# Reordering the loads, writes and small matmuls at the start of a fused SSM-convolution and GeGLU kernel

## The chip, the cores and the metric

The kernel runs on one core of a Trainium2 chip. The metric is the device time of one execution in microseconds (us); less is better. The kernel before was timed three times: 909.62, 912.13 and 916.34 us, median 912.13. One more execution was profiled.

## What is computed

Two layers, one after the other, are each applied twice to x (2048 tokens by 576 channels, bf16): a gated long convolution and a feed-forward block. Cut to what matters:

```python
def _A_ref(q, k, v, shift_k, ssm_k, ssm_D):       # q is layernorm(x)
    k_shift = sum over t of k delayed by t, times shift_k[:, ks - 1 - t]     # ks = 4 taps
    kv = k_shift * v
    y = irfft(rfft(kv, 2S) * rfft(ssm_k, 2S))[:S]  # causal convolution along the tokens, per channel
    return q * (y + kv * ssm_D)

def _B_ref(x, w_gate, w_up, w_down):              # 576 -> 4608 -> 576
    return (gelu(x @ w_gate) * (x @ w_up)) @ w_down

x = A_q
x = x + _A_ref(layernorm(x), A_k, A_v, A_shift_k, A_ssm_k, A_ssm_D)
x = x + _B_ref(layernorm(x), B_w_gate, B_w_up, B_w_down)
x = x + _A_ref(...); x = x + _B_ref(...)
```

The convolution y does not depend on x, so it is computed once and used by both layers.

## The kernel before, in words

**Tiling.** Tokens are worked on in four blocks of 512. The convolution of a block is done by transforms that are matmuls with tables of cosines and sines (W, Wx); the product with the transformed filter stands in between, on VectorE (DVE). Filter block b is needed from token block b on. The feed-forward block runs in units (layer, token block), each in three phases of 12 feature tiles; weights for the gate and up products come in groups of four tiles (a group, wgu, is three loads: L1193 to L1195), down weights in halves of a phase (wd, L1203). TensorE (PE) carries nearly everything.

**Who orders the work.** Each engine runs its instructions in program order. The start (function begin, L831 to L1130) is written out by hand. After it a planner takes over: it keeps a model of the engines' times (Pace) and, between the feed-forward products, calls fill (L1420), which hands out the waiting convolution steps, loads and writes as the model says that they are ready. Loads and writes are issued by SP (nc.sync) and by POOL (nc.gpsimd), a few small ones by ACT (nc.scalar); each of these queues issues in order, and a DMA that has to wait holds up all that stand behind it on the same queue.

**The start.** SP loads k, the first filter block hn, v, the tables, x_b (L863 to L875), and then weight groups 0 and 1 (L876, head.more(1)). ACT loads the taps as one row, sk1 (L862), and the vector D as one row, dvec (L864). TensorE turns the tap row into columns with twelve matmuls of one column each (L891), which become wcol (L894); from wcol DVE and ACT make diagonal matrices dg, and with them the shift of k by its taps is done on TensorE (shift_taps, L818). The last 192 channels are shifted on DVE instead (L943 to L949) with sx, the taps broadcast by two matmuls (L906, L909). D becomes columns by five one-column matmuls (L915), goes to dcol (two copies, L933 and L934) and is added to the filter's first tap (L939). Then k*v (L991) and the first filter block (hT0) are transformed (L219, L228), multiplied (kacc) and transformed back (L415).

**The second filter block.** It has to be turned so that its time steps lie on the partitions. Four transposing DMAs read it from DRAM into hx[:, 0] (L977); SP then issues weight group 2 (L978, head.more(2)), writes hx[:, 0] to DRAM (Td, L979), and reads it back in another order into hx[:, 1] (L981). The tile hx takes over the place of kT, the shifted k's operand, so the first transpose waits for kT's last reader. Its transform (L282) is put between the feed-forward products by the planner; the first of these comes after the seventh product of the first unit.

**Writes and POOL's queue.** put(kt, ...) writes transformed blocks to DRAM, h0[kt] to Hd and kc[kt] to Kd (spill, L425): put(0, h0, kc), put(2, h0), put(2, kc), then the taps' broadcast skc (L1083), k of token block 1 (load_k(1), L1084), put(1, h0, kc), put(3, h0), v of block 1 (L1094), put(3, kc). They are read again in the steps of later token blocks (kr, hr; L547, L555).

**The first unit.** The first unit's first phase is done in two halves of 256 tokens, six products (half_gu, L1673, 36 matmuls each) per half, since token tiles 0 and 2 are normalised first. first_half (L1601) does the six products of tiles 0 and 2; after the third and the fourth of them (n = 2 and 3) tiles 1 and 3 are turned (turn0, nine transposes on TensorE, L1478) and copied by ACT (copy0, two copies, L1485), for the second half. The fifth product is the first to use weight group 2, the third the first to use group 1. Products n < 4 are finished by a Gelu on ACT and a multiplication on DVE (L1678, L1679); later ones by two ACT instructions (hidden, L1652 and L1653) and a multiplication over two products on DVE (L1656). PSUM pairs of the products come from a pool of three, in turn; the turnings take from the same pool.

Of the kernel before, what the change touches and what calls it, by code (L numbers as in the profile page):

```python
# [18 lines left out]
BF16 = mybir.dt.bfloat16  # L19
# [3 lines left out]
P = 128  # L23
# [63 lines left out]
class Conv:  # L87
# [743 lines left out]
    def begin(self, head, tables):  # L831

        tc, nc, D, KS = self.tc, self.nc, self.D, self.KS
        nd = D // P
        width = lambda db: min(P, D - db * P)
        with ExitStack() as es:
            tmp = es.enter_context(tc.tile_pool(name="s_tmp", bufs=1))
            AT = 96
            sk1 = tmp.tile([AT + 1, D, KS], BF16, name="sk1")
            dvec = tmp.tile([1, D], BF16, name="dvec")  # L840
            dcol = tmp.tile([P, nd + 1], F32, name="dcol")
            nt = nd - 1
            DW = D - nt * P
# [13 lines left out]
            full = wx[1][:].rearrange("p i c -> p (i c)")[:, 0:256]  # L857

            nc.vector.memset(full, 1.0)
            nc.vector.memset(ones[:], 1.0)  # L860
            nc.vector.memset(sk1[0:AT, nt * P:, :], 0.0)
            nc.scalar.dma_start(out=sk1[AT:AT + 1, :, :].rearrange("p d j -> p (d j)"), in_=self.sk.rearrange("d j -> (d j)").unsqueeze(0))  # L862
            self.load_k(0, nc.sync)  # L863
            nc.scalar.dma_start(out=dvec[:], in_=self.sD.unsqueeze(0))  # L864
            nc.vector.memset(kT[:, :, :, 0:2], 0.0)
            nc.vector.memset(below[:, 0:1], 0.0)
            nc.vector.tensor_copy(out=below[:, 1:P], in_=self.ident[:, 0:P - 1])
# [5 lines left out]
            head.more(0)  # L873
            nc.sync.dma_start(out=self.Wx[:], in_=tables[:, 24:26, :])
            nc.sync.dma_start(out=self.W[:, 12:24, :], in_=tables[:, 12:24, :])  # L875
            head.more(1)  # L876

            new = lambda: self.psp.tile([P, 2, 512], F32, tag="pr", name="ps")
            small = lambda: self.cpsp.tile([P, 2, 512], F32, tag="cps", name="cps")
# [6 lines left out]
            idle = small()  # L886
            busy(idle, 8)
            ps = new()
            for db in range(nt):
                for j in range(KS):  # L890
                    nc.tensor.matmul(ps[:, 0, db * KS + j:db * KS + j + 1], lhsT=sk1[AT:AT + 1, db * P:(db + 1) * P, j],  # L891
                                     rhs=ones[AT:AT + 1, 0:1],
                                     start=True, stop=True)
            nc.vector.tensor_copy(out=wcol[:].rearrange("p b j -> p (b j)"), in_=ps[:, 0, 0:nt * KS])  # L894

            def diagonals(db, js=range(KS)):
                for j in js:
# [13 lines left out]
            rest = slice(nt * P, D)  # L911
            px = new()
            at = DW
            for db in range(nd + 1):
                nc.tensor.matmul(px[0:width(db), 1, at + db:at + db + 1], lhsT=dvec[:, db * P:db * P + width(db)], rhs=ones[0:1, 0:1],  # L915
                                 start=True, stop=True)
            for i in range(KS - 1):
                nc.tensor.matmul(px[:, i // 2, i % 2 * DW:(i % 2 + 1) * DW], lhsT=below[:], rhs=k[:, RT - KS + 1 + i, rest],
                                 start=True, stop=True)
# [2 lines left out]
            for n, dbs in enumerate(DBS):  # L922
                pt = new_t() if n else small_t()
                pts.append(pt)
                for e, db in enumerate(dbs):
                    for u in range(RT):
                        nc.tensor.transpose(pt[:, e, u * P:(u + 1) * P], k[:, u, db * P:(db + 1) * P], self.ident[:])
            nc.scalar.copy(out=kx[:, 0:2, :], in_=px[:, 0, 0:2 * DW].rearrange("p (i c) -> p i c", c=DW))
            nc.scalar.copy(out=kx[:, 2, :], in_=px[:, 1, 0:DW])
            for dbs, pt in zip(DBS, pts):  # L930
                ne = len(dbs)
                if dbs is DBS[1]:
                    nc.scalar.copy(out=dcol[:, 0:nd], in_=px[:, 1, at:at + nd])  # L933
                    nc.scalar.copy(out=dcol[0:D - nd * P, nd:nd + 1], in_=px[0:D - nd * P, 1, at + nd:at + nd + 1])  # L934
                nc.scalar.copy(out=kT[:, dbs[0]:dbs[-1] + 1, :, 2:P + 2],
                               in_=pt[:, 0:ne, 0:RT * P].rearrange("p e (u q) -> p e u q", u=RT))

# [37 lines left out]
            hx = head.scratch([P, 2, RT, D], "hx")  # L975
            for i in range(RT):
                nc.sync.dma_start_transpose(out=hx[:, 0, i:i + 1, :], in_=self.hk[:, BS + i * P:BS + (i + 1) * P])  # L977
            head.more(2)  # L978
            nc.sync.dma_start(out=self.Td[1].rearrange("(t p) d -> p t d", p=P), in_=hx[:, 0])  # L979
            self.hT1 = hx[:, 1]  # L980
            nc.sync.dma_start(out=self.hT1, in_=self.Td[1].rearrange("(p i) d -> p i d", i=RT))  # L981
            skT = tc.dram_tile([1, KS * D], BF16, name="skT")
# [1 line left out]
            def taps_out():  # L984
                for j in range(KS):
                    nc.gpsimd.tensor_copy(out=self.skc[AT:AT + 1, j, :], in_=sk1[AT:AT + 1, :, j])
                nc.gpsimd.dma_start(out=skT[:], in_=self.skc[AT:AT + 1, :, :].rearrange("p j d -> p (j d)"))
            for dbs, o in zip(DBS, out):
                ne = len(dbs)
                vd = v[:, :, dbs[0] * P:(dbs[0] + ne) * P].rearrange("p i (e c) -> p e i c", e=ne)  # L990
                tt(out=vd, in0=o[:, 0:ne], in1=vd, op=ALU.mult)  # L991
# [29 lines left out]
            def put(kt, *what):  # L1021
                for w in what:
                    self.spill((self.Kd if w is kc else self.Hd)[0][kt], w[kt])
                self.flush(0.0)
# [56 lines left out]
            whole(1, 1)  # L1081
            kfwd(1, 1, new())
            nc.gpsimd.dma_start(out=self.skc[:].rearrange("p j d -> p (j d)"), in_=skT[:].broadcast_to([P, KS * D]))  # L1083
            self.load_k(1, nc.gpsimd)  # L1084
            apart(1, 0)
            apart(1, 1)
            kacc(1)
            put(1, h0, kc)
            put(3, h0)
            head.even_out(0)  # L1090
            kfwd(3, 0, small())
            head.even_out(2)
# [11 lines left out]
            for j in (0, 2):  # L1104
                head.gate_even(j, Y[j])
                head.mean(j)
            put(3, kc)
            for j in (0, 2):
                head.sq(j)
                head.std(j)  # L1110
# [16 lines left out]
            head.stats(3)  # L1127
            head.gate(1, None, 0)
            self.A0 = A
            self.startup = False  # L1130


@with_exitstack
def ssm_geglu_kernel(ctx, tc, A_q, A_k, A_v, A_shift_k, A_ssm_k, A_ssm_D, B_x, B_w_gate, B_w_up,
# [53 lines left out]
    def load_wgu(n):  # L1188
        if n >= NWB * GP:
            return  # L1190
        f0 = (n % NG) * fw
        w = wpool.tile([P, NKC, fw], BF16, tag="wgu", name="wgu")
        nc.sync.dma_start(out=w[0:HK, :, :], in_=wg_v[:, :, f0:f0 + fw])  # L1193
        nc.sync.dma_start(out=w[HK:P, 0:NKC - 1, :], in_=wu_v[:, 1:NKC, f0:f0 + fw])
        nc.sync.dma_start(out=w[HK:P, NKC - 1:NKC, :], in_=wu_v[:, 0:1, f0:f0 + fw])  # L1195
        wgu[n] = w
# [248 lines left out]
    with tc.manual_schedule():  # L1445
# [24 lines left out]
        def turn0(j, other=None):  # L1470
            if 0 not in xnT_of:
                xnT_of[0] = xtp.tile([P, NKC, CH], BF16, tag="xnT", name="xnT")
            if j not in turned:
                reserve0(j, other)
            pt = turned[j]
            for b in range(NKC):
                c0 = b * P if b < 5 else HK + (b - 5) * P
                nc.tensor.transpose(pt[b // 5][:, b // 5, (b % 5) * P:(b % 5 + 1) * P], xn0[j][:, c0:c0 + P], ident[:])  # L1478
# [103 lines left out]
        def more(k):  # L1582
            if k == 0:
                load_x(0, nc.sync)
            elif k == 1:
                for n in range(2):
                    load_wgu(n)
            else:
                load_wgu(2)
        head = SimpleNamespace(  # L1590
            zero=neghalf_t[:], more=more, reserve=reserve0, idle=idle0, stats=stats0, act_stats=act_stats0, half_stats=half_stats0, root_of=root_of0, mean_of=mean_of0, scales=scales0, even_out=even_out0, gate_even=gate_even0, gate=gate0, mean=mean0, sq=sq0, std=std0, norm=norm0, turn=turn0, copy=copy0,
            scratch=lambda shape, name: xtp.tile(shape, BF16, tag="xnT", name=name),
# [8 lines left out]
        def first_half(hT):  # L1601

            gvars[0][1]["rstd"] = small.tile([P, 1], F32, tag="e_rstd", name="rstd")
            nc.vector.reciprocal(out=gvars[0][1]["rstd"][:], in_=gvars[0][1]["std"])
            gate0(1, None, 1)
            mean0(1)
            gate0(3)
            mean0(3)
            for n in range(FP // 2):
                tail = half_gu(hT, n, 0, n < 4)  # L1610
                t.pe += C_GU
                if n == 3:
                    t.on_dve(C_HT, t.on_act(C_GELU, t.pe + 0.15) + 0.15)
                if n == 0:
                    sq0(1)
                    root0(1)
                    norm0(1)
                if n < 4:
                    tail()
                if n == 1:  # L1620
                    sq0(3)
                    load_x(1)
                    root0(3)
                elif n in (2, 3):
                    if n == 2:
                        norm0(3)
                        for part, kt in ((1, 0), (0, 1), (1, 1)):
                            conv.apart0(conv.A0, part, kt)
                        conv.together0(conv.A0)
                        t.dve, t.act = t.pe + 2.4, t.pe + 0.6  # L1630
                    conv.run_p()
                    j = 2 * n - 3
                    turn0(j)
                    copy0(j, nc.scalar.copy)
                    t.on_act(1.4, t.pe)
                if n > 3:
                    tail()
                if n == 4:
                    t.dve -= EARLY
                if n > 1:  # L1640
                    fill(t.pe + C_GU + HURRY, False, True)
# [67 lines left out]
        for wb, ph, ui, first, final in visits:  # L1709
# [27 lines left out]
            if wb == 0:  # L1737
                first_half(hT)
                for n in range(FP // 2):
                    tail = half_gu(hT, n, 1, False)  # L1740
                    t.pe = max(t.pe, free.popleft()) + C_GU
                    free.append(tail())
                    if n == 0:
                        conv.window = t.pe + 0.6
                    if n % 2:
                        when_due(t.pe, load_wgu, n // 2 + 3)
                    fill(t.pe + lead(FP // 2 - 1 - n), now(), conv.left > 0)
# [135 lines left out]
```

## Time and profile before

| | |
|---|---|
| median of three runs | 912.13 us |
| profiled execution, its own time | 916.24 us |
| its span, first to last instruction | 914.3 us |
| PE busy | 902.3 us, 99% of the span |
| DVE, ACT, POOL busy | 63%, 36%, 18% |
| weight loads of PE (PEld) busy | 57% |
| DMA | 132.90 MB, mean 145 GB/s |

Times in the profile are counted from the span's start. A row of the list of waits has who waited, for what, the total in us, how often, and the longest. A row of the timeline has start, length, engine, line, operation and tiles; in brackets the idle time before it and what ended it. The list of DMA issues gives the size of each and the median time from issue to landing. The chain of work that ended last is followed back from the last instruction, each step to what released it.

### The profile page before, as it was taken

How to read it: one execution, taken by the hardware profiler on the slowest of the kernel's cores; microseconds unless marked ns; L12 is line 12 of the kernel's file. 1: busy time of each engine (PE TensorE's matmuls, PEld its weight loads, DVE VectorE, ACT ScalarE, POOL GpSimd, SP SyncE). 2: the span in 40 equal slices, each digit the busy share in tenths (PEclk: the TensorE clock that was granted, in tenths of full speed). 3: DMA queues.
4: the chain of work that ended last, by engine and by line, in shares of the span. 5: the costliest groups of instructions: out<-in, count | busy, mean ns of one | idle time of the engine just before them, and what ended most of it. 6: DMA issues, size and time to landing. Idle time of an engine off the chain costs nothing.

```text
span 914.3 us, 19185 instructions
## 1 busy us (share of the span) xinstructions
PE 902.3 (99%) x8143; PEld 525.5 (57%) x8143; DVE 576.8 (63%) x985; ACT 328.9 (36%) x618; POOL 160.2 (18%) x339
## 2 busy tenths in 40 slices
PE   9979999999999999999999999999999999999998
PEld 7766556465565564664655655646646546556555
DVE  8978987679788885697898855443333335333332
ACT  7745534633324255353124133551121224321211
POOL 4502504220114031330114002220000003100000
PEclk9999999999999999999999999999999999999999
DMA  9999995938428508784915700870620721967620
GB/s 250 329 265 236 281 264 116 230 130 195 157 80 226 144 14 150 228 156 99 278 54 127 189 10 32 179 153 20 137 79 2 155 79 27 180 161 175 140 59 27
DMA packets 132025, 132.90 MB, mean 145 GB/s; under 512 B 46114, under 2 KB 123619, under 8 KB 131940
## 3 DMA queue, kind: packets, MB, share of 16 engines
q1 hardware_dynamic: 121728, 94.65, 46.2%
q0 software_dynamic: 10208, 37.02, 12.7%
q8 instruction: 63, 1.03, 0.5%
q14 instruction: 22, 0.18, 0.1%
q10 hardware_dynamic: 4, 0.01, 0.0%
HBM read 108.35 MB, written 12.39 MB: 132 GB/s over the span
## 4 chain that ended last, share of the span: by engine, by line
PE 94%; DMA 4%; DVE 1%; SPq 1%; ACT 0%; issue 0%; ACTq 0%
PE gu L1755 59%; PE dn L1789 31%; DMA Td<-hx 2%; PE gu L1673 1%; DMA hx<-Td 1%; PE cps L282 1%; SPq L977 1%; PE ps L282 1%; DMA hx<-in_A_ssm_k_dram 0%; PE ps L415 0%; PE cps L415 0%; PE cps L885 0%; DVE v L991 0%; DVE wx L948 0%; DVE wx L947 0%; ACT h L1010 0%
## 5 line engine op out<-in xcount | busy, mean ns | idle before, releaser
L1755 PE MATMUL gu<-xnT,wgu 64*128 64x512 bf16 x4968 | 540.7, 377 | 0.0
L1755 PEld LDWEIGHTS <-wgu 64*128 64x128 bf16 x4968 | 240.1, 94 | 293.9 <-issue 6.2
L1764 ACT ACTIVATE ga<-gu 128x512 f32<-128x512 f32 x258 | 153.9, 596 | 451.1 <-PE gu L1755 442.7
L1765 DVE TENSOR_TENSOR hT<-ga,gu 128x512 bf16<-128x512 f32 x258 | 177.1, 687 | 200.4 <-ACT ga L1764 198.9
L1789 PE MATMUL dn<-wd,hT 128*128 128x288 bf16 x2304 | 292.2, 287 | 0.0
L1789 PEld LDWEIGHTS <-hT 128*128 128x128 bf16 x2304 | 223.4, 98 | 65.7 <-issue 9.5
L1828 DVE TENSOR_TENSOR x_c<-x_c,dn 128x576 f32<-128x576 f32 x62 | 46.7, 753 | 55.2 <-PE dn L1789 54.9
L1231 POOL TENSOR_SCALAR nm<-s 128x1 f32<-128x1 f32 x56 | 20.1, 358 | 267.4 <-DVE x_c L1820 210.8
L1239 ACT ACTIVATE junk<-x_c,nm 128x576 bf16<-128x576 f32 x48 | 36.9, 769 | 28.4 <-POOL nm L1231 25.9
L1247 POOL TENSOR_TENSOR rstd<-ve,neghalf_t 128x1 f32<-128x1 f32 x58 | 37.5, 647 | 4.8
L555 POOL DMA_DIRECT2D hr<-Hd x32 | 17.4, 545 | 118.0 <-DVE prod L361 118.0
L1303 ACT ACTIVATE xn<-x_c,nb,rstd 128x576 bf16<-128x576 f32 (+1 forms) x48 | 28.6, 644 | 5.9 <-POOL nb L1251 5.7
L285 ACT COPY eo<-cps 128x576 f32<-128x576 f32 x29 | 18.6, 642 | 31.6 <-PE cps L282 28.3
L1246 POOL TENSOR_SCALAR ve<-ss 128x1 f32<-128x1 f32 x58 | 21.3, 367 | 47.2 <-ACT junk L1239 47.1
L1811 DVE TENSOR_TENSOR ob<-x_c,dn 128x576 bf16<-128x576 f32 x15 | 11.3, 754 | 29.0 <-PE dn L1789 29.0
L1652 ACT ACTIVATE ga<-gu 128x512 bf16<-128x512 f32 x26 | 15.5, 597 | 34.5 <-PE gu L1755 25.9
L1673 PE MATMUL gu<-xnT,wgu 64*128 64x256 bf16 x432 | 26.3, 279 | 0.6 <-ACT xnT L1485 0.6
L1673 PEld LDWEIGHTS <-wgu 64*128 64x128 bf16 x432 | 22.0, 98 | 4.4 <-issue 1.4
L362 DVE TENSOR_TENSOR prod<-prod 128x576 bf16<-128x576 bf16 x48 | 22.0, 458 | 1.7
L430 POOL DMA_DIRECT2D out_dram<-ob x12 | 6.8, 563 | 91.8 <-issue 47.0
L245 DVE SCALAR_TENSOR_TENSOR eo<-eo 128x576 f32<-128x576 f32 x22 | 16.3, 753 | 5.8 <-ACT eo L285 5.8
L1281 DVE SCALAR_TENSOR_TENSOR x_c<-g_t,rstd,x_c 128x576 f32<-128x576 f32 x16 | 13.0, 815 | 8.6 <-POOL rstd L1247 8.6
(188 smaller groups left out, 589.9 us busy)
## 6 DMA issues: line engine op xcount, KB each, us to landing
wgu<-in_B_w_gate_dram SPq DMA_DIRECT2D x45, 576.0 KB, 5.6
wd<-in_B_w_down_dram SPq DMA_DIRECT2D x30, 864.0 KB, 6.8
wgu<-in_B_w_up_dram SPq DMA_DIRECT2D x45, 512.0 KB, 7.9
hr<-Hd POOLq DMA_DIRECT2D x32, 288.0 KB, 4.8
kr<-Kd POOLq DMA_DIRECT2D x24, 288.0 KB, 5.0
Kd<-kc POOLq DMA_DIRECT2D x12, 288.0 KB, 6.3
k<-in_A_k_dram POOLq DMA_DIRECT2D x3, 1008.0 KB, 13.5
wgu<-in_B_w_up_dram SPq DMA_DIRECT2D x45, 64.0 KB, 7.4
```

The lines of the kernel that those rows point to most:

```text
L362: nc.vector.tensor_tensor(out=dst, in0=pr[:, 0, :], in1=pr[:, 1, :], op=ALU.subtract if part == 0 else ALU.add)
L1231: nc.gpsimd.tensor_scalar(out=v["nm"][:], in0=v["s"][:], scalar1=-1.0 / D, scalar2=None, op0=ALU.mult)
L1239: nc.scalar.activation(out=junk[:], in_=get_x(), func=ACT.Square, bias=v["nm"][:, 0:1], accum_out=v["ss"][:])
L1246: nc.gpsimd.tensor_scalar(out=ve[:], in0=v["ss"][:], scalar1=1.0 / D, scalar2=EPS, op0=ALU.mult, op1=ALU.add)
L1247: nc.gpsimd.tensor_tensor(out=v["rstd"][:], in0=ve[:], in1=neghalf_t[:, 0:1], op=ALU.pow)
L1303: nc.scalar.activation(out=xn[:, lo:hi], in_=x_c[c][:, j, 0:hi - lo], func=ACT.Identity, scale=v["rstd"][:, 0:1], bias=v["nb"][:, 0:1])
L1673: nc.tensor.matmul(pair[:, s, e * 256:(e + 1) * 256], lhsT=w[r0:r0 + HK, k, gi * P:(gi + 1) * P], rhs=xnT[r0:r0 + HK, blk_of[k], tok], sta ...
L1755: nc.tensor.matmul(pair[:, s, :], lhsT=w[r0:r0 + HK, k, gi * P:(gi + 1) * P], rhs=xnT[r0:r0 + HK, b, :], start=(k == 0), stop=(k == NKC - 1))
L1764: nc.scalar.activation(out=ga[:], in_=pair[:, 0, :], func=ACT.Gelu_apprx_tanh)
L1765: nc.vector.tensor_tensor(out=hT[:, fi, :], in0=ga[:], in1=pair[:, 1, :], op=ALU.mult)
L1789: nc.tensor.matmul(part[h][:, h, 0:HW], lhsT=hT[:, fi, at * P:(at + 1) * P], rhs=wd[2 * wb + fi // WT][:, fi % WT, h * HW:(h + 1) * HW], s ...
L1828: nc.vector.tensor_tensor(out=xh, in0=xh, in1=acc[:, :, 0:HW], op=ALU.add)
```

## The change

Five edits, all at the start of the kernel:

- The taps are loaded a second time, as three rows of 128 channels (sk3), by ACT right after k's load has been issued by SP. Four matmuls of three columns each take the place of the twelve for wcol. dvec becomes a tile of five rows of 128 that is cleared first and loaded by two DMAs; one matmul, now behind the transposes of k, gives all of D's columns, and one copy takes the place of two for dcol.
- SP issues the four transposes before any weights; then weight group 0, then the Td write, then groups 1 and 2, then the read-back.
- k of token block 1 is loaded by POOL right after the taps have been written to DRAM, ahead of all puts.
- The writes of kc[1], h0[3] and kc[3] leave the start; put_rest issues them in the third step (n = 2) of the first unit's second half.
- Tiles 1 and 3 are turned after the fourth and the fifth product of the first half, not after the third and the fourth.

```diff
+            sk3 = tmp.tile([nd - 1, P, KS], BF16, name="sk3")
-            dvec = tmp.tile([1, D], BF16, name="dvec")
+            dvec = tmp.tile([nd + 1, P], BF16, name="dvec")
...
+            nc.vector.memset(dvec[:], 0.0)
...
             self.load_k(0, nc.sync)
-            nc.scalar.dma_start(out=dvec[:], in_=self.sD.unsqueeze(0))
+            nc.scalar.dma_start(out=sk3[:], in_=self.sk[0:nt * P, :].rearrange("(b p) j -> b p j", p=P))
+            nc.scalar.dma_start(out=dvec[0:nd, :], in_=self.sD[0:nd * P].rearrange("(b p) -> b p", p=P))
+            nc.scalar.dma_start(out=dvec[nd:nd + 1, 0:D - nd * P], in_=self.sD[nd * P:D].unsqueeze(0))
...
             nc.sync.dma_start(out=self.W[:, 12:24, :], in_=tables[:, 12:24, :])
-            head.more(1)
...
-            for db in range(nt):
-                for j in range(KS):
-                    nc.tensor.matmul(ps[:, 0, db * KS + j:db * KS + j + 1], lhsT=sk1[AT:AT + 1, db * P:(db + 1) * P, j],
-                                     rhs=ones[AT:AT + 1, 0:1],
-                                     start=True, stop=True)
-            nc.vector.tensor_copy(out=wcol[:].rearrange("p b j -> p (b j)"), in_=ps[:, 0, 0:nt * KS])
+            for j in range(KS):
+                nc.tensor.matmul(ps[:, 0, j * nt:(j + 1) * nt], lhsT=sk3[:, :, j], rhs=self.ident[0:nt, 0:nt], start=True, stop=True)
+            nc.vector.tensor_copy(out=wcol[:], in_=ps[:, 0, 0:nt * KS].rearrange("p (j b) -> p b j", b=nt))
...
-            for db in range(nd + 1):
-                nc.tensor.matmul(px[0:width(db), 1, at + db:at + db + 1], lhsT=dvec[:, db * P:db * P + width(db)], rhs=ones[0:1, 0:1],
-                                 start=True, stop=True)
...
+            nc.tensor.matmul(px[:, 1, at:at + nd + 1], lhsT=dvec[:], rhs=self.ident[0:nd + 1, 0:nd + 1], start=True, stop=True)
...
-                    nc.scalar.copy(out=dcol[:, 0:nd], in_=px[:, 1, at:at + nd])
-                    nc.scalar.copy(out=dcol[0:D - nd * P, nd:nd + 1], in_=px[0:D - nd * P, 1, at + nd:at + nd + 1])
+                    nc.scalar.copy(out=dcol[:], in_=px[:, 1, at:at + nd + 1])
...
                 nc.sync.dma_start_transpose(out=hx[:, 0, i:i + 1, :], in_=self.hk[:, BS + i * P:BS + (i + 1) * P])
+            head.more(1)
+            nc.sync.dma_start(out=self.Td[1].rearrange("(t p) d -> p t d", p=P), in_=hx[:, 0])
             head.more(2)
-            nc.sync.dma_start(out=self.Td[1].rearrange("(t p) d -> p t d", p=P), in_=hx[:, 0])
...
                 nc.gpsimd.dma_start(out=skT[:], in_=self.skc[AT:AT + 1, :, :].rearrange("p j d -> p (j d)"))
+                self.load_k(1, nc.gpsimd)
...
-            self.load_k(1, nc.gpsimd)
...
-            put(1, h0, kc)
-            put(3, h0)
+            put(1, h0)
...
-            put(3, kc)
...
+            def put_rest():
+                put(1, kc)
+                put(3, h0, kc)
+            self.put_rest = put_rest
...
             elif k == 1:
-                for n in range(2):
-                    load_wgu(n)
+                load_wgu(0)
             else:
-                load_wgu(2)
+                for n in range(1, 3):
+                    load_wgu(n)
...
-                elif n in (2, 3):
+                elif n in (2, 3, 4):
...
-                    conv.run_p()
-                    j = 2 * n - 3
-                    turn0(j)
-                    copy0(j, nc.scalar.copy)
-                    t.on_act(1.4, t.pe)
+                    if n < 4:
+                        conv.run_p()
+                    if n > 2:
+                        j = 2 * n - 5
+                        turn0(j)
+                        copy0(j, nc.scalar.copy)
+                        t.on_act(1.4, t.pe)
...
+                    elif n == 2:
+                        conv.put_rest()
```

More of the change, by code (lines that the diff above doesn't have):

```diff
@@ L1585, in more @@
             elif k == 1:
-                for n in range(2):
+                load_wgu(0)
+            else:
+                for n in range(1, 3):
                     load_wgu(n)
-            else:
-                load_wgu(2)
         head = SimpleNamespace(
```

## The prediction

> **What bounds the kernel now.** I read the profile's first two parts (busy times and slices), then the busy times of chosen stretches, then TensorE's waits, then the chain of work that ended last in its order of time, and last the queues' issues. The stretches (their columns: length, then busy time and instruction count of PE, PEld, DVE, ACT and POOL, the granted clock, the DMA engines' busy share, GB/s) say where time can be won at all:
>
> ```profile
> 12.00:20.00 8.00, 7.72 (x64) 6.09 (x63) 7.49 (x18) 6.11 (x12) 5.91 (x10) 1.00 1.11 221
> 24.40:47.00 22.60, 20.37 (x292) 17.63 (x291) 20.62 (x50) 15.64 (x33) 13.11 (x23) 1.00 1.07 337
> 55.40:58.80 3.40, 3.40 (x33) 2.23 (x32) 0.00 (x0) 1.18 (x2) 0.00 (x0) 0.50 1.08 389
> 62.00:914.00 852.00, 848.97 (x7533) 483.05 (x7531) 526.34 (x870) 289.84 (x543) 135.60 (x290) 1.00 0.56 135
> ```
>
> From 62 us to the end TensorE is busy 849 of 852 us. So whatever the change does, it does by moving the moment at which TensorE passes 62 us; its waits before that are these, all of them:
>
> ```profile
> PE cps L282 <- DMA hx<-Td: 4.9, 1, 4.9
> PE cps L885 <- DVE wx L859: 1.2, 1, 1.2
> PE xps L1478 <- DVE hT L1679: 0.9, 1, 0.9
> PE ps L415 <- DVE yb L362: 0.8, 1, 0.8
> PE gu L1673 <- ACT xnT L1485: 0.6, 1, 0.6
> PE cps L219 <- DVE v L991: 0.3, 1, 0.3
> ```
>
> One is large: the first matmul of the second filter block (L282) waits for its turned data. The chain shows why they are late:
>
> ```profile
> 27.21 19.40 DMA Td<-hx
> 46.61 0.02 issue
> 46.62 8.34 DMA hx<-Td
> 54.96 0.04 issue
> 55.01 0.40 PE cps L282 x2
> 55.41 0.39 PE ps L282 x2
> 55.80 3.54 PE gu L1673 x36
> ```
>
> The round trip through DRAM (write Td, read it back) lasts 27.8 us, and after the wait the 36 products take 3.54 us. At full clock 108 of them take 6.07 us (row below), 2.02 us for 36. The stretch 55.4 to 58.8 stands at clock 0.50, so the wait costs 4.94 us and then 1.52 us: 6.46 us is the most that curing this wait can give.
>
> But the DMA share in both early stretches is above 1.0: all 16 engines are full. Moving one transfer forward moves another back. That is the question here.
>
> **Filter block ahead of the weights.** The four transposes write a tile that takes over kT's place, so they wait for its last reader, L818:
>
> ```profile
> 10.07 1.05 PE L818 MATMUL ps<-dg,kT 128*128 128x512 bf16 x7
> ```
>
> ```profile
> 66.54 1.20 SPq L455 DMA_TRANSPOSE hb<-in_A_ssm_k_dram  x1
> ```
>
> That is 11.12 us, and 12.1 with the later start worked out below. Issued without backlog a transpose takes SP 1.20 us (second row); four are through at 16.9. Weight group 0 follows at once. SP then stands at the Td write until the transposes have landed; groups 1 and 2, the read-back and the three down-weight loads are queued behind that wait. It costs nothing, since group 0 keeps the engines occupied. What it costs is that from 12 to about 17 us nothing but transposes is in flight, while before 1.8 MB of weights went through in the stretch 12 to 20. I let the weights flow from 18.5 us, between the end of issuing (16.9) and that plus a few us for the transposes ahead of them.
>
> What has to be moved before group 2 has landed, in the sizes of these rows:
>
> ```profile
> k<-in_A_k_dram POOLq DMA_DIRECT2D x1, 1008.0 KB, 13.5
> Hd<-h POOLq DMA_DIRECT2D x3, 288.0 KB, 13.9
> wgu<-in_B_w_gate_dram SPq DMA_DIRECT2D x1, 576.0 KB, 7.2
> skc<-skT POOLq DMA_DIRECT2D x1, 576.0 KB, 11.2
> Td<-hx SPq DMA_DIRECT2D x1, 576.0 KB, 19.4
> v<-in_A_v_dram POOLq DMA_DIRECT2D x1, 576.0 KB, 16.0
> x_b<-in_A_q_dram POOLq DMA_DIRECT2D x1, 576.0 KB, 7.7
> yb<-yb POOLq DMA_DIRECT2D x4, 144.0 KB, 5.0
> ...
> wgu<-in_B_w_up_dram SPq DMA_DIRECT2D x1, 512.0 KB, 14.3
> wgu<-in_B_w_up_dram SPq DMA_DIRECT2D x1, 64.0 KB, 14.6
> ```
>
> Three groups of 1152 KB, k 1008, five writes of 288, and 576 each for skc, Td, v, x_b and the four yb: 8784 KB, 9.0 MB. The mixed stretch runs at 337 GB/s, weights alone (12 to 20) at 221. If all of it ran mixed: 26.7 us, landed at 45.2. If all three groups (3.54 MB) ran alone: 16.0 and 16.2 us, landed at 50.7. I take 2.0 MB alone (group 0 before and after k, some of group 1 while POOL's queue is empty): 29.8 us, so **48.3 us**.
>
> When is group 2 needed? By the fifth product of the first half:
>
> ```profile
> 43.39 0.68 PE L1478 MATMUL xps<-ident,xn 128*128 128x128 bf16 x9
> 43.99 6.07 PE L1673 MATMUL gu<-xnT,wgu 64*128 64x256 bf16 x108
> ```
>
> It starts at 43.99 now; the change takes one turning from in front of it (0.60), and the terms below add 1.4: 44.8. So TensorE waits 3.5 us for weights. Group 1 is needed two products, one turning and the 0.9 us wait earlier, at 39.2; by the same sums (6.64 MB up to it, 1.5 MB alone) it lands at 40.6. So the wait falls in two parts, 1.4 and 2.1 us, each under the 4.94 after which the clock fell; I count no slow clock. Bounds: 0.4 and 5.9 us.
>
> The Trainium skill, "DMA: Bandwidth & Descriptors", section "Issuing engines are not separate DMA queues", says that transfers issued by different engines run on the same 16 DMA engines and interleave. It speaks against this change, since k's earlier load on POOL's queue then takes its share from group 0. If POOL's transfers were free, three groups and Td would need 12.2 us and there would be no wait for weights; by the rule the 3.5 us above stand. The trace agrees: Td's 576 KB took 19.4 us beside POOL's writes and loads.
>
> **Columns by five matmuls.** Twelve one-column matmuls and five more become four and one. TensorE was not short there, but the new operand sk3 is loaded second on ACT's queue, in the place where dvec was:
>
> ```profile
> 3.06 0.47 PEld L891 LDWEIGHTS <-sk 1*128 1x128 bf16 x12 [0.41 <-issue]
> 3.54 0.13 PEld L906 LDWEIGHTS <-ones 97*128 97x128 bf16 x2
> 4.30 0.32 PEld L915 LDWEIGHTS <-dvec 1*128 1x128 bf16 x5 [0.62 <-DMA dvec<-in_A_ssm_D_dram]
> ```
>
> The first operand was there by 3.06, dvec only at 4.30. So the tap columns start 1.24 us later and take some 0.3 us less: **+1.0 us** (bounds 0.2, if sk3 lands with sk1, and 1.5, if three rows take longer than one). Behind it stand wcol, the diagonals, sx and the chain on DVE up to v (L991), for which TensorE already waits (0.3 us in the list of waits), so it passes in full to L219. The dvec memset, a fourth small DMA and one copy less on ACT lie beside this.
>
> **k's load.** POOL issues it after the taps, one issue earlier than Wn and the scales:
>
> ```profile
> 26.16 0.54 POOL L176 DMA_DIRECT2D k<-in_A_k_dram  x1
> ```
>
> POOL is the next to full in these stretches (5.91 of 8 us), so I take it as a chain, and its scales for L1538 come 0.54 later; behind that on ACT stands the copy of kc for the last products, and behind those the 0.8 us wait of L415. **+0.4 us** (bounds 0 and 0.54).
>
> **Three writes later.** 864 KB leave the full stretch; that is in the list above already. They are issued in the second half's third step, near 62 us, when POOL has nothing else to do. The tiles that they hold are rewritten from here on:
>
> ```profile
> L254 DVE TENSOR_TENSOR kc<-eo x8: 452/454/458, 74.2 to 85.7; 128x288 bf16<-128x288 f32 x8
> ```
>
> 12 us cover them; in the full stretch such a write took 13.9, there the engines are less full. I count 0; without the cover DVE would stand some 2 us at 74, and TensorE would feel what its PSUM pairs do not buffer.
>
> **Two tiles turned a step on.** The turnings cost TensorE the same 0.6 us each. But the second one's copies now stand on ACT in front of the Gelu pair of the fifth product, whose PSUM pair the second half's first product takes over (three pairs in turn):
>
> ```profile
> 44.10 1.18 ACT L1485 COPY xnT<-xps 128x640 bf16<-128x640 bf16 x2
> 46.18 0.60 ACT L1652 ACTIVATE ga<-gu 128x512 bf16<-128x512 f32 x1 [0.90 <-PE gu L1673]
> 46.67 0.58 ACT L1653 CAST hT<-gu 128x512 bf16<-128x512 f32 x1
> ```
>
> From the fifth product's end: 0.71 to the copies' start (43.39 to 44.10), 1.18, then 1.07 for the pair, 0.1 to hand over: 3.06 us. TensorE covers 0.60 + 2.02 = 2.62. **+0.45 us** (bounds 0 and 0.6). The wait of 0.9 for hT stays: now the fourth product takes that pair.
>
> **Sum.** -4.94 - 1.52 + 1.0 + 0.4 + 3.5 + 0.45 = **-1.1 us**. The read-back follows group 2 in its queue with 0.6 MB beside it: 1.2 MB, landed near 52, while L282 is reached at 48.3 + 2.02 + 3.06 + 2.02 = 55.4. The sum is against the profiled execution, 916.24 us (span 914.3); the median of the three runs, 912.13, is 4.1 lower. I set the change against the median: **911.0 us**.
>
> **The rivals.** *Weights in time* (no weights alone): the wait is 0.4 and the change gives -4.2 us: 907.9. For it speak the 389 GB/s of the stretch 55.4 to 58.8; against it the 221 GB/s of weights alone. *Slower, by the clock:* if the weights flow at 221 GB/s throughout, the wait is 5.9, and if it falls in one gap as long as the 4.94 that halved the clock, 1.5 us are added: +2.8 us, 914.9. It decides once the average falls below about 300 GB/s. The Trainium skill, "TensorE: Matmul & The Clock Gate", section "What's actually happening", gives half clock after an idle window of about 3.4 us, with a window that runs free; by that rule two gaps of 1.4 and 2.1 would not trip it and one of 4 may. The row at 0.50 agrees, being 3.4 us long. *The filter block is last all the same:* if the read-back still takes its 8.34 us, counted from 48.3, L282 waits 1.2 us: 912.2.
>
> **How the numbers follow.** My sum 0.40, weights in time 0.22, slower by the clock 0.25, filter block still last 0.13. The range 906.5 to 916.5 takes in all four and leaves out some 2 in 10, for the 4 us by which the profiled run stands off the median. Within 1% (902.9 to 921.3, about what a measurement of this kernel can tell from no change) lie all four cases: faster 0.02, same 0.94, slower 0.04.
>
> **What would show it.** TensorE's waits: L282 on hx gone, two new ones of L1673 on the wgu loads with 3.5 us together, PEclk 1.00 throughout, the wait of L415 slightly longer, the second half's first product waiting for ACT's hT. wcol 1 us later. Td's write landing in clearly less than 19.4 us, and hx before L282. I am wrong if L1673 never waits for a load, if the clock falls in a weights wait, or if TensorE waits anywhere after 62 us.

## The result and the profile after

The changed kernel takes 919.39 us (median of nine, 917.69 to 920.57), the kernel before 912.13 (nine, 909.62 to 916.34): ratio 1.0067, 95% interval 1.0042 to 1.0091. It is slower, where 911.0 was forecast, and outside the range. The profiled execution took 920.57 us (span 918.8), 4.33 more than the profiled one before. In three kernels below (e6, e8, e9) single executions lie anywhere between 909.6 and 935 us, and a ratio would compare only the undisturbed ones, so for these the median and the spread stand instead. The executions of the kernel before lay between 909.6 and 918.2 in all.

TensorE's waits up to 62 us, changed kernel (after 62 us there is none, as before):

```profile
PE gu L1676 <- DMA wgu<-in_B_w_gate_dram: 2.6, 1, 2.6
PE gu L1676 <- DMA wgu<-in_B_w_up_dram: 2.3, 1, 2.3
PE ps L893 <- DMA sk<-in_A_shift_k_dram: 1.8, 1, 1.8
PE cps L888 <- DVE dvec L861: 1.2, 1, 1.2
PE pt L954 <- ACT dcol L931: 0.8, 1, 0.8
PE ps L415 <- DVE yb L362: 0.8, 1, 0.8
PE gu L1676 <- ACT xnT L1486: 0.6, 1, 0.6
```

The wait for hx is gone, and weight waits stand in its place, as forecast. The chain that ended last, in order of time, shows a second thing, which was not:

```profile
1.28 3.57 DMA sk<-in_A_shift_k_dram
4.85 0.05 issue
4.89 0.29 PE ps L893 x4
...
10.59 3.41 PE cps L818 x14
```

The three-row tap operand lands at 4.85 us. TensorE's fourteen shift matmuls then take 3.41 us by the chain, and the first product with v starts at 16.12 us instead of 12.37. The same work in TensorE's timeline, the kernel before and then the changed one (rows left out between):

```profile
7.98 1.91 PE L818 MATMUL cps<-dg,kT 128*128 128x512 bf16 x14
...
12.37 1.14 PE L219 MATMUL cps<-v,W 128*128 128x288 bf16 x8 [0.28 <-DVE v L991]
```

```profile
10.39 3.62 PE L818 MATMUL cps<-dg,kT 128*128 128x512 bf16 x14
...
16.12 1.14 PE L219 MATMUL cps<-v,W 128*128 128x288 bf16 x8
```

TensorE's timeline of the changed kernel later on:

```profile
44.20 0.28 PE L1676 MATMUL gu<-xnT,wgu 64*128 64x256 bf16 x1 [2.57 <-DMA wgu<-in_B_w_gate_dram]
46.74 6.52 PE L1676 MATMUL gu<-xnT,wgu 64*128 64x256 bf16 x71 [2.25 <-DMA wgu<-in_B_w_up_dram]
53.19 0.68 PE L1479 MATMUL xps<-ident,xn 128*128 128x128 bf16 x9
53.80 2.56 PE L1676 MATMUL gu<-xnT,wgu 64*128 64x256 bf16 x36
```

The two waits are both for group 1 (its gate part, then its up part), with a single matmul between them. Two stretches of the changed kernel, columns as before:

```profile
12.00:20.00 8.00, 8.00 (x59) 5.56 (x58) 6.09 (x14) 3.97 (x8) 2.65 (x5) 1.00 0.28 39
```

```profile
47.00:50.60 3.60, 3.60 (x38) 2.51 (x36) 0.00 (x0) 0.00 (x0) 0.00 (x0) 0.50 1.10 237
```

Between 12 and 20 us the DMA engines moved 39 GB/s at a share of 0.28, where the kernel before moved 221 at 1.11. And after the weight waits the clock was half. SP's queue says why the engines were idle:

```profile
6.80 0.33 SPq L879 DMA_DIRECT2D W<-twiddles  x1
15.38 6.31 SPq L974 DMA_TRANSPOSE hx<-in_A_ssm_k_dram  x4
```

From 7.1 to 15.4 us SP stood before the first transpose, which needs kT's place, with all weights behind it.

### The profile page after: what moved, and what is told of

It is laid out like the page before. It is cut to its first block, busy times and chain, and to the rows that moved or that the text cites. A ratio compares the mean times of both kernels' runs of the same rounds, so it can differ in the third digit from the quotient of the medians.

```text
span 918.8 us, 19168 instructions
## 1 busy us (share of the span) xinstructions
PE 905.2 (99%) x8131; PEld 525.7 (57%) x8131; DVE 576.9 (63%) x986; ACT 328.6 (36%) x617; POOL 159.9 (17%) x339
## 3 DMA queue, kind: packets, MB, share of 16 engines
q0 software_dynamic: 10208, 37.02, 12.1%
## 4 chain that ended last, share of the span: by engine, by line
PE 95%; DMA 2%; SPq 2%; ACT 0%; issue 0%; ACTq 0%; DVE 0%
PE gu L1760 59%; PE dn L1794 31%; DMA wgu<-in_B_w_up_dram 2%; PE gu L1676 2%; PE cps L282 1%; SPq L1196 1%; SPq L974 1%; PE ps L282 0%; PE ps L415 0%; PE cps L415 0%; SPq L1195 0%; DMA sk<-in_A_shift_k_dram 0%; PE cps L818 0%; SPq L1194 0%; PE pt L954 0%; PE ps L818 0%
## 5 line engine op out<-in xcount | busy, mean ns | idle before, releaser
L1833 DVE TENSOR_TENSOR x_c<-x_c,dn 128x576 f32<-128x576 f32 x62 | 46.6, 752 | 55.3 <-PE dn L1794 54.9
L1247 POOL TENSOR_SCALAR ve<-ss 128x1 f32<-128x1 f32 x58 | 21.3, 367 | 47.3 <-ACT junk L1240 47.2
```

The source lines that it names most:

```text
L1247: nc.gpsimd.tensor_scalar(out=ve[:], in0=v["ss"][:], scalar1=1.0 / D, scalar2=EPS, op0=ALU.mult, op1=ALU.add)
L1833: nc.vector.tensor_tensor(out=xh, in0=xh, in1=acc[:, :, 0:HW], op=ALU.add)
```

## The experiments

Each edit is against the kernel named. The ratio is to the kernel before, measured beside it on the same chip; medians of the kernel before were 911.5 in the first set of runs (e1 to e4), 914.06 in the second (e5 to e8) and 913.79 in the third (e9 to e12).

Three names recur in the expectations. The *clock theory* says that TensorE's gap in front of the late columns costs more than its own length, as TensorE comes to full speed later; the *operand theory* says that it costs its length alone. *Starved engines* means that the DMA engines stand idle while SP waits to issue the transposes, and that this makes the weights late.

**e1, the columns alone**, in the kernel before: sk3, the five matmuls and the rows of dvec.

> The kernel before with the edit of the columns alone (sk3, the five matmuls, dvec in rows). Clock theory: TensorE stands still from 3.1 us until sk3 lands near 4.9, and full clock, which the kernel before has from 7.6 us, comes one or two windows of 3.4 us later; the first product with v (L219 in the kernel before, 12.4 us) starts near 16. Operand theory: only the late operand counts, 1.6 us, and L219 starts near 14. Either way the wait for the second filter block, which does not hang on TensorE, shrinks by what the start loses (4.9 to about 1 by the clock theory, to 3.3 by the other), so that the time is within 3 us of the kernel before.

912.21 us, ratio 0.9992 (0.9973 to 1.0011). The first product with v starts at 15.48 us, as the clock theory has it, and the shift matmuls take 3.47. So the start loses 3.1 us, and the time does not change: in this profile no wait for hx is left.

**e2, the changed kernel without the columns.**

> The changed kernel without the edit of the columns (order, k's load, writes, turnings stay). Clock theory: L219 starts near 12.4 instead of 16.1, the transposes near 12 instead of 15.4, weights and need both move 3.5 us earlier, the waits for weights stay near 5 us, and the time is 3 to 4 us under the changed kernel's 919.4: about 916. Operand theory: 1.6 us, about 918. If the columns cost nothing: 919.

916.32 us, ratio 1.0031 (1.0010 to 1.0052): 3.1 us under the changed kernel, as the clock theory has it. L219 starts at 12.82, the transposes at 12.07, and TensorE still waits 5.4 us for weights.

**e3, the changed kernel, TensorE kept busy.**

```diff
-            busy(idle, 8)
+            busy(idle, 16)
```

> The changed kernel with sixteen warming matmuls instead of eight in front of the columns, so that TensorE has no gap between 3.1 us and sk3's landing; the operand is as late as before. Clock theory: full clock again by about 7.6 us, L219 near 14, the time 2 us or more under 919.4. Operand theory: the columns still start near 4.9, L219 stays near 16, the time stays at 919 or goes up.

916.82 us, ratio 1.0039 (1.0018 to 1.0059). TensorE's timeline (rows left out between):

```profile
1.24 3.59 PE L888 MATMUL cps<-wx 128*128 128x256 bf16 x16 [1.24 <-DVE dvec L861]
4.77 0.29 PE L893 MATMUL ps<-ident,sk 3*128 3x3 bf16 x4
...
8.98 1.91 PE L818 MATMUL cps<-dg,kT 128*128 128x512 bf16 x14
...
13.82 0.41 PE L219 MATMUL cps<-v,W 128*128 128x288 bf16 x2 [0.72 <-DVE v L990]
```

The operand is as late as before, yet the shift matmuls need 1.91 us instead of 3.62, and L219 starts at 13.82 instead of 16.12. Eight more matmuls that compute nothing won 2.6 us. Of the start's loss of 3.75 us, 2.3 are thus the clock; the other 1.45 are the late operand and whatever else the columns cost.

**e4, the order of SP's queue alone**, in the kernel before.

> The kernel before with the order of SP's queue alone (transposes, group 0, Td, groups 1 and 2). Theory of the starved engines: L219 near 12.4 as in the kernel before; the DMA engines stand nearly idle between 12 us and the transposes' landing; the wait for hx is gone and two waits for weight groups of together 4 to 7 us stand in its place, with half clock after them; POOL's three writes and k's load compete as before, so the time is 914 to 918. Theory that the order is good and the columns alone did the harm: 908 to 911.

919.88 us, ratio 1.0070 (1.0045 to 1.0094), worse than expected: the order alone costs as much as the whole change. TensorE's waits, and a stretch of the same run:

```profile
PE gu L1673 <- DMA wgu<-in_B_w_gate_dram: 4.6, 1, 4.6
PE gu L1673 <- DMA wgu<-in_B_w_up_dram: 4.4, 2, 3.2
```

```profile
48.00:58.00 10.00, 4.37 (x39) 2.99 (x41) 4.73 (x7) 0.00 (x0) 1.23 (x3) 0.50 1.10 299
```

Nine us of waits for groups 1 and 2, and half clock throughout these 10 us. The waits are longer than e2's 5.4 us; which of the edits that e2 has besides (k's early load, the late writes, the turnings) helps it was not tried singly.

**e5, the changed kernel with SP's queue as before.**

> The changed kernel with SP's queue as before (groups 0 and 1, then the transposes, group 2, Td); columns, k's load, writes and turnings stay. Theory of the starved engines (the order is the cause): no wait for weight groups, no half clock in the first half, the DMA engines full from 10 us on; the time falls by about 8 us to 910 to 912. If the order mattered only together with the late columns: 915.

912.89 us, ratio 0.9989 (0.9969 to 1.0009), 6.5 us under the changed kernel, and no wait for weights or hx. e4 and e5 agree: the order does the harm, with the columns or without them.

**e6, Td's write ahead of group 2 only**, with POOL's part of the change (groups 0 and 1 stay ahead of the transposes).

> The kernel before with three small moves: Td's write ahead of group 2 only (groups 0 and 1 stay ahead of the transposes), k's load early, the three writes late. Starved engines: they stay full, Td lands by 38 us instead of 46.6, the wait of L282 for hx is gone, group 2 lands by 44 us; the time is 909 to 911, under the median of the kernel before. If each transfer moved forward pushes back another by as much: a wait for group 2 of 3 us or more, 913 to 915.

The median is 924.16 us, the spread 909.57 to 934.97. Neither theory had said this. **e8, POOL's part alone**:

> The kernel before with POOL's part alone (k's load early, three writes late). 864 KB leave the stretch in which Td's write is under way: it lands 2 to 3 us earlier than at 46.6, the wait for hx falls from 4.9 to 2 us or less and the clock does not fall: 909.5 to 911.5. If k's early load costs group 1 or the transposes as much: no change, 912.

The median is 922.0 us, the spread 910.12 to 926.99. Some executions are as fast as I hoped, most far slower; what the two kernels share is POOL's part. The third set of runs took it apart.

**e9, k's early load alone**, in the kernel before:

```diff
                 nc.gpsimd.dma_start(out=skT[:], ...)
+                self.load_k(1, nc.gpsimd)
...
-            self.load_k(1, nc.gpsimd)
```

> The kernel before with k's early load alone. Theory of the jam: k's 1 MB in 8 KB pieces, issued on POOL near 17.6 us, meets the transposes in flight; the engines fall to some 60 GB/s for several us, the transposes need about 20 us to land instead of 4 to 8, and most runs take 920 us or more, as in the run of POOL's part alone. Rival, the late writes did that: this kernel stays at 910 to 916.

The median is 920.42 us, the spread 910.19 to 932.60: eight of its twelve executions took 919 us or more, and of the 110 of the kernel before none took more than 918.24. So this edit, alone, is enough. Issues of the profiled execution (919.9 us) from 14 to 24.4 us, with the median time from issue to landing at the end:

```profile
k<-in_A_k_dram POOLq DMA_DIRECT2D x1, 1008.0 KB, 12.5
Hd<-h POOLq DMA_DIRECT2D x1, 288.0 KB, 13.8
wgu<-in_B_w_up_dram SPq DMA_DIRECT2D x1, 64.0 KB, 12.9
hx<-in_A_ssm_k_dram SPq DMA_TRANSPOSE x4, 14.8
```

The transposes need 14.8 us, in the kernel before 6.4; Td's write is issued at 39.38 us, there at 27.21. TensorE then waits 3.1 us for hT, 2.8 for a weight load and 1.6 for hx. The edit does not always do this: two of the twelve executions took 910.2 us. And e5, which has it too, shows no execution over 914.4 us, although k's load and the transposes are in flight together there as well (they land after 8.6 us):

```profile
14.49 9.22 SPq L975 DMA_TRANSPOSE hx<-in_A_ssm_k_dram  x4
```

```profile
20.41 0.59 POOL L176 DMA_DIRECT2D k<-in_A_k_dram  x1
```

In the profiled executions of the four kernels that load k early and keep weights ahead of the transposes, these landed the later, the sooner k's load followed the first of them: 5.9 us behind in e5 (8.6 us to landing), 3.8 in e9 (14.8), 3.3 in e8 (19.5), 2.0 in e6 (20.2). That is one execution of each kernel, a hint and not a rule.

**e10, Td first and late writes, but k's load where it was**:

> The kernel before with Td's write ahead of group 2 and the three late writes, k's load where it was. Theory of the jam: without k's load beside the transposes no run is over 917; Td lands by 40 us, no wait for hx, 909.5 to 911.5. Rival, the late writes or Td's place did it: runs of 920 to 935 come again.

914.25 us, spread 910.22 to 917.44, ratio 0.9993 (0.9972 to 1.0015): no execution beyond those of the kernel before, so the late writes and Td's place do not make the slow executions. But there is no gain either: a wait for group 2 of 2.1 us takes the place of that for hx, and although it is that short, the clock is half after it (columns of the second view as before):

```profile
46.59 7.73 PE L1676 MATMUL gu<-xnT,wgu 64*128 64x256 bf16 x107 [2.14 <-DMA wgu<-in_B_w_up_dram]
```

```profile
46.60:50.00 3.40, 3.40 (x34) 2.47 (x36) 3.23 (x6) 0.00 (x0) 2.13 (x4) 0.51 1.12 271
```

The 107 matmuls take 1.7 us longer than at full clock (6.0).

**e11, the turnings alone**, in the kernel before.

> The kernel before with the two turnings a step later, alone. If the prediction's term holds, the second half's first product waits 0.45 us for ACT's copies; in a kernel that waits for hx right after, this is hidden: 910 to 916 as the kernel before. If the turnings cost more, a wait over 1 us on ACT stands in front of that product.

912.9 us, ratio 0.9997 (0.9977 to 1.0017). No wait stands in front of the second half's first product. A new one stands in front of the second turning, and the 0.9 us wait for hT is now that of the fourth product:

```profile
45.85 0.66 PE L1478 MATMUL xps<-ident,xn 128*128 128x128 bf16 x9 [0.33 <-DVE hT L1681]
```

From the first product (33.64 us here, 33.65 in the kernel before) the first seven products and both turnings end at 50.55 us instead of 50.06, so the turnings cost 0.5 us there. The wait for hx behind them, 0.75 us in this profile, hides it.

**e7, a buffer of their own for the transposes**, in the changed kernel without the columns:

```diff
+            hx0 = tmp.tile([P, RT, D], BF16, name="hx0")
...
-                nc.sync.dma_start_transpose(out=hx[:, 0, i:i + 1, :], ...)
+                nc.sync.dma_start_transpose(out=hx0[:, i:i + 1, :], ...)
...
-            nc.sync.dma_start(out=self.Td[1].rearrange(...), in_=hx[:, 0])
+            nc.sync.dma_start(out=self.Td[1].rearrange(...), in_=hx0[:])
```

> The changed kernel without the edit of the columns, and with the transposes writing a buffer of their own instead of kT's place, so that they need not wait for kT's last reader. Starved engines: the transposes are issued near 6 us instead of 12, the weights flow from 12 us instead of 18, groups 1 and 2 land some 5 us earlier, the waits for them shrink from 5.4 to under 1 us, and the time falls from 916.3 to 909 to 911. If the order itself is the cause, through the bytes put ahead of group 2: the waits stay at 4 us or more, 915 to 917.

910.99 us (910.42 to 911.41), ratio 0.9962 (0.9942 to 0.9982). The order is that of e2, which is 5.3 us slower; only the transposes' wait for kT is gone. They are issued from 4.77 us:

```profile
4.77 8.16 SPq L977 DMA_TRANSPOSE hx<-in_A_ssm_k_dram  x4
12.98 0.66 SPq L1197 DMA_DIRECT2D wgu<-in_B_w_gate_dram  x1
```

```profile
PE gu L1679 <- DMA wgu<-in_B_w_up_dram: 0.7, 1, 0.7
```

The weights' wait falls from 5.4 to 0.7 us, and the clock stays at 1.00. So putting the filter block first is sound; what ruins it is that it waits, and the weights with it.

**e12, the same with k's load back behind skc.**

> The kernel with the transposes' own buffer (order, late writes, turnings, no columns), with k's load back behind skc. If k's early load matters only where it meets transposes in flight, nothing changes here, since they have landed by 17 us: 910.5 to 911.5. If it delays the weights, this kernel is up to 1 us faster and its wait for the weights (0.7 us) is gone.

910.34 us (910.14 to 910.70), ratio 0.9959 (0.9945 to 0.9973), the fastest and steadiest kernel here. It is faster than both kernels of this case; the 0.65 us to e7 were measured on different chips and prove nothing by themselves. TensorE's waits (all of its list):

```profile
PE cps L885 <- DVE wx L860: 1.2, 1, 1.2
PE gu L1679 <- DVE hT L1685: 1.0, 1, 1.0
PE ps L415 <- DVE yb L362: 0.7, 1, 0.7
PE gu L1679 <- ACT xnT L1489: 0.6, 1, 0.6
PE xps L1482 <- DVE hT L1685: 0.3, 1, 0.3
```

No DMA stands in it any more, so the 0.7 us wait for the weights is gone, as the second of the expectations says.

## Why the prediction was wrong, point by point

Three steps failed: the price of the columns, the clock after the weight waits, and the execution that the gain was counted from. That weights would come late was foreseen, but that term was 1.7 us too small.

*The wait for hx goes (-4.94 and -1.52).* Right against the profiled execution; against the median see the end.

*"TensorE was not short there", columns +1.0 us.* Wrong: +3.75 us. This is the first step that failed. 1.45 us remain in e3, near the upper bound of 1.5: sk3 landed at 4.85, while I took dvec's 4.30. The other 2.3 us are the clock. I treated the gap in front of the columns as idle time that costs only itself, but it fell into TensorE's warm-up (the time at the start before it runs at full speed). The 3.75 are the far end of a range: without the columns, and apart from e4, which waits for hn there, L219 starts between 12.37 and 12.94 us and the shift matmuls take 1.91 to 2.73; with them, in the changed kernel, e1 and e5, it starts between 15.23 and 16.12 and they take 3.47 to 3.62. The time that e2 wins, 3.1 us, is the better figure. Also, what should "lie beside this" did not: the copy of kx now waits for the dvec matmul, as it stands behind the transposes, and the filter's turning for dcol:

```profile
7.84 0.48 ACT L926 CAST kx<-ps 128x384 bf16<-128x384 f32 x1 [0.92 <-PE ps L925]
```

```profile
9.58 1.01 PE L954 MATMUL pt<-ident,hn 128*128 128x128 bf16 x8 [0.80 <-ACT dcol L931]
```

*Transposes at 12.1 us.* They were issued at 15.38, since kT's last reader was late by the step above; without the columns at 12.07.

*Weights: 3.5 us of waiting, bounds 0.4 and 5.9.* Measured 2.57 + 2.25, and 0.4 in the fifth product (2.56 instead of 2.14): 5.2 us; without the columns 5.4. The mechanism was right and the size within its bounds, but too small. The weights flowed from 21.73 us instead of 18.5, and group 2 landed 32.45 us after that instead of 29.8, at 54.18 instead of 48.3; from 21.7 to 54.2 us the engines moved 291 GB/s, where my sum has 302. The need moved back too, but less: group 1 was needed at 41.6 us instead of 39.2, and its last part landed at 46.7 instead of 40.6.

*"The wait falls in two parts, each under 4.94; I count no slow clock".* Wrong: the second step that failed. The two parts were not a wait for group 1 and, two products later, one for group 2. Both were for group 1, one matmul apart, 4.8 us together. The clock fell, which I had named as a sign of being wrong, and the 71 matmuls after the waits took 6.52 us instead of 3.98: +2.5. Nor would two separate waits have been safe: I took 4.94 us as the length after which the clock falls, and in e10 a wait of 2.14 us was enough. The rival that is slower by the clock named this mechanism; it had the wait as a single gap at group 2, and did not have the clock at the start.

*k's load +0.4.* From L219 to the first product of the first half it was 21.28 us and is 21.33: +0.05. That this edit could stall the transposes was missing altogether. In the changed kernel it did not show; there the transposes had landed by 24.4 us, soon after k's load was issued (21.3); in the kernel before, its single executions are the slowest of any edit made alone (e9).

*Writes 0.* Right: in the changed kernel TensorE waits nowhere after 62 us. *Turnings +0.45.* In the changed kernel 0, behind the weight waits; in e11, where no weights are late, 0.5, so the size was right, but TensorE waits in front of the second turning, for DVE, and not in front of the second half's first product, for ACT. The wait of 0.9 for hT stayed in e11, at the fourth product as I said; in the changed kernel it vanished behind the weight waits.

The measured terms: -6.46 + 3.80 + 5.2 + 2.5 - 0.9 = +4.1, and 0.2 more for the lone matmul between the two waits (0.28 us instead of 0.06); TensorE reaches L282's second visit at 63.61 instead of 59.27, +4.34, and the profiled executions differ by 4.33. The medians differ by 7.3, since the profiled execution before was among the slower ones of its kernel. This is the third step that failed: I set my sum against the median without asking why the two differed by 4.1 us. In e11's profiled execution, 910.92 us, TensorE waits 0.75 us for hx and the clock stays at 1.00. Of the 101 executions of the kernel before beside e1 to e12, the 36 under 912 us have a mean clock of 0.999 or more, the 39 over 915 us one of 0.998 or less. So much of the gain that I counted is probably not there in the faster executions; none of them was profiled. Why the wait comes and goes from one execution to the next is not settled.

## What to carry to other kernels

Before a transfer is moved to the head of a queue, look for what it waits for: whoever stands behind it waits too, and when the queue was the one that kept the engines full, the loss is all the bytes of that time. Give such a transfer a buffer of its own first; the order may then be right. And when small work at a kernel's start is saved or its operand comes later, check that the matrix engine's warm-up stays unbroken: here eight idle matmuls were worth 2.6 us.

## What the runs showed of the hardware that was not expected

A gap of 1.8 us in the warm-up was enough to keep TensorE at about half speed until about 14 us: fourteen shift matmuls take 3.62 us against 1.91 without the gap. (A second gap, 0.8 us for dcol, falls into the same time; e3 has one like it, but is at full speed by then.) The Trainium skill, "TensorE: Matmul & The Clock Gate", section "What's actually happening", has full clock only after some 3.4 us of sustained work; e3 agrees: it works from 1.24 us on without a gap, and its three matmuls of L915 take 0.41 us at 5.41 us, in the changed kernel 0.69 at 5.72. The profile's granted clock reads 1.00 in that stretch all the same; only the durations tell.

Two waits of 2.6 and 2.3 us with one matmul of 0.28 us between them halved the clock as one long wait does (0.50 from 47 to 50.6 us). In e10 a single wait of 2.14 us did so, behind nine short transposes and one matmul (0.51 from 46.6 to 50 us); in e11 waits of 0.92 and 0.75 us did not (1.00 from 40 to 55 us).

A load of 1 MB on POOL's queue beside four transposing loads on SP's made them land after 14.8 us instead of 6.4 (e9), but after 8.6 where it came later behind them (e5). In e9 the engines were about as busy from 24 to 30 us as in the kernel before (0.97 against 1.02), yet moved 185 GB/s against 284; what was in flight differed, and what in the engines does this was not tried.
